# Decode of float64 weights: scales on ScalarE alone, subtracts on VectorE alone, one reduction for the sums of attention weights, and other prices in the planner

## The chip, the core and the metric

The kernel runs on one core of a Trainium2 chip. A core has a matrix engine (TensorE, in rows PE, its weight loads PEld), three engines for elementwise work (VectorE or DVE, ScalarE or ACT, GpSimd or POOL), and an engine that issues transfers (SyncE or SP). Each engine works through its own instructions strictly in order, and waits where an instruction needs the result of another engine or of a transfer. The metric is device microseconds (us) for one execution; lower is better. TensorE's clock has two levels, 1.2 and 2.4 GHz; the profile prints the granted clock as a share of the upper one.

## What is computed

Causal attention with a cumulative bias, then two feed-forward layers over the same 2304 tokens (4 batches of 576):

```
scores = scale * q @ k.T                      # 4 batches, 8 heads, 576 tokens, 64 wide
cum    = cumsum(max(s, 0))
scores = where(causal, -1e9, scores + min(-(cum_i - cum_j), 0))
attn   = exp(scores - max(scores))
attn   = attn / (sum(attn) + 1e-9)
x      = (attn @ v) as (2304, 512)
x      = ((x @ w_a) * (x @ w_b)) @ w_out      # 512 -> 1536 -> 512
out    = (relu(x @ w_in) ** 2) @ w_out2       # 512 -> 2048 -> 512
```

The weights of both layers come as float64. The kernel reads each one as two 32-bit words and makes a float32 pair of it, a high part and a low part.

## The kernel before, in words

All matrix products that need it are made from pairs: high x high, high x low, low x high. That keeps TensorE busy; everything else exists to feed it.

*Decode.* For each tile of 128 x 512 weights a transfer brings 512 KB of raw words (rows `roomxh`, `roomxl`, `words` in the first layer, `v_0r`, `v_1r` in the second). `decode` then scales the high word by 2^-112, shifts it and combines it with its sign (into `t`; rows `roomxl`, `wt`, `v_0t`, `v_1t`), scales the low word by 2^-29, adds both on GpSimd, rounds the sum to the high part (`wh`, `w2h`) on ScalarE, and subtracts that from the sum for the low part (`wl`, `wlo`, `w2l`). Its last argument says which engines may do the subtract: P is GpSimd, D is VectorE. The first layer has 36 such tiles (12 steps f of w_a, w_b and w_out), the second 32. Low parts of the first layer are also written to DRAM (`wlab`, `wlo`) and read back by later chunks (`lo`, `loo`). Raw words of the first 24 tiles rotate through six buffers, those of the last twelve through three.

*Attention.* Batch 0 is done in two parts (256 and 320 queries), the others whole. For each head: scores (`st`), maxima on VectorE (`neg`), exponentials on ScalarE with their sums (`e`, `tot`, in rows `sum`), 1e-9 added and the reciprocal on VectorE (`one`), the weights scaled by it, transposed on TensorE (`pt`), split (`ph`, `pl`) and multiplied with the values (`av`). Where a row of scores lies in two banks, its two sums are added first.

*Feed-forward.* The first layer goes over tokens in chunks; the first chunk (256 tokens) takes its weights directly as they are decoded (`ab`, then `py`). The second layer runs at the end, 512 tokens at a time (`ph`, `po`).

*Order.* `Plan` records every operation with the engines that may do it, a cost for each, and whether it uses the port that VectorE and GpSimd share (third field of a way). `Plan.order` then plays the operations through: for each engine it takes the first startable one by rank (on TensorE attention before feed-forward, elsewhere the reverse), chooses the engine where it can start first, keeps at most one user of the shared port at a time (`port`), and lets the transfers queue up to 3 us ahead of a modelled DMA (`dma`, `QUEUE`). Only the order is emitted; on the chip nothing waits for the planner's times.

Nearly all instructions are issued in line 246, so rows are told apart by their tiles.

Of the kernel before, what the change touches and what calls it, by code (L numbers as in the profile page):

```python
# [248 lines left out]
def attention_moe_moe(tc, q, k, v, s, w_a, w_b, w_out, w_in2, w_out2, out):  # L249
# [73 lines left out]
    def on_dve(method, n, *args, two=False, each=1.04, **kw):  # L323
        return "DVE", 150 + each * n, two, method, args, kw
# [7 lines left out]
    def dve(*args, reads=(), **kw):  # L332
        pl.call(on_dve(*args, **kw), reads=reads)
# [4 lines left out]
    def gps(*args, **kw):  # L338
        pl.call(on_gps(*args, **kw))

    def dma(out, in_, kb, takes=(), lag=0.0):
        pl.call(("SP", kb * 3.0, False, "dma_start", (out, in_), {}), takes=takes, lag=lag)
# [33 lines left out]
    def at_const(shape, dtype, name):  # L376
        v = pl.fixed(lambda: pools["at"].tile(shape, dtype, name=name))
        v.buf.gate = swapped
        return v
# [75 lines left out]
    for i in range(4):  # L455
        t = [at_const([P, NJ + 2], F32, f"{z}{i}") for z in ("neg", "sum", "one")]
        for x in t:
            gps("memset", NJ + 2, x, 1.0)
        small.append(t)
# [110 lines left out]
    def softmax(b, p, h, q0, qn, head):  # L570
# [10 lines left out]
        for i, pieces in enumerate(banks):  # L581
# [53 lines left out]
            for blk, k0, m, to, kn, ee in held:  # L635
                c = blk if k0 == 0 else nq
                n_ = nq + 1 if halves else blk
                act(
                    "activation", kn + 360, ee.part((blk, k0)), to, AF.Exp, bias=neg[:m, n_ : n_ + 1].part(n_),
                    accum_out=tot[:m, c : c + 1].part(c), psum=True,  # L640
                )
            held = []
        if banks[-1][0][1]:
            dve("tensor_reduce", 2, out=tot[:, nq - 1 : nq], in_=tot[:, nq - 1 : nq + 1], op=ALU.add, axis=AX.X)
        qs = slice(first_block, nq)
        dve("tensor_scalar_add", nq, one[:, qs], tot[:, qs], 1e-9)
# [133 lines left out]
    def decode(w, by_col, f, hi, lo, nm, raw, t, takes, by):  # L780
# [5 lines left out]
        else:  # L786
# [7 lines left out]
        pl.call(  # L794
            on_dve("tensor_scalar", n, hf, hf, 2.0**-112, None, op0=ALU.mult, each=0.52),
            on_act("mul", n, hf, hf, 2.0**-112),
        )
        dve("tensor_scalar", n, t, high, 3, 0x7FFFFFF8, op0=ALU.logical_shift_left, op1=ALU.bitwise_and, each=0.52)
        dve("scalar_tensor_tensor", n, t, high, -0x80000000, t, op0=ALU.bitwise_and, op1=ALU.bitwise_or, two=True)
        pl.call(  # L800
            on_act("activation", n, low, low.bitcast(U32), AF.Copy, scale=2.0**-29),
            on_dve("tensor_scalar", n, low, low.bitcast(U32), 2.0**-29, None, op0=ALU.mult, each=0.52),
        )
# [11 lines left out]
    def split_w(f):  # L815
        def g():
# [5 lines left out]
            for i, w in enumerate((w_a, w_b, w_out)):  # L822
# [10 lines left out]
                decode(w, i < 2, f, hi, lo, f"w{f}_{i}", words[k_ % len(words)], t, (), "PD")  # L833
# [275 lines left out]
```

## Time and profile before

| | |
|---|---|
| runs (us) | 1162.74, 1163.14, 1169.74; median 1163.14 |
| profiled execution (us) | 1163.58, its span 1161.8 |
| mean granted clock of TensorE | 0.964 |
| busy TensorE | 1105.1 us (95%) |
| busy VectorE | 670.9 us (58%) |
| busy ScalarE | 494.9 us (43%) |
| busy GpSimd | 324.3 us (28%) |
| transfers | 143.85 MB, mean 124 GB/s |

The span is the time from the first to the last instruction. Busy times are unions; matmuls are pipelined, so a busy TensorE need not be at its peak. Shares over the whole span mix stages: decode and attention of batch 0 first, then attention beside the first layer, then the first layer alone, then the second decode and the second layer. Rows are therefore given by stretches of time. A group's row gives its instructions (x), busy us, mean ns of one, and after the second bar the idle time of the engine just before them with what ended it.

### The profile page before, as it was taken

To read this page: it belongs to the slowest core of one execution; us is meant where nothing else is said; L and a number is where in the kernel's file an instruction comes from. 1 tells how busy PE (TensorE), PEld (TensorE's weight loads), DVE (VectorE), ACT (ScalarE), POOL (GpSimd) and SP (SyncE) were. 2 spreads that over 40 slices of the span, in tenths; PEclk is the share of its full clock that TensorE was granted. 3 is DMA by queue.
4 is the path that set the end of the run, shared out by engine and by line. 5 is a ranking of instruction groups with operands and counts; after the bars stand their busy time and mean duration, and the time that the engine had idled before them with its cause. 6 is when DMAs were issued, how large, how long until landed. Compare 5 with 4: busy or idle time off the path is not lost.

```text
span 1161.8 us, 16590 instructions
## 1 busy us (share of the span) xinstructions
PE 1105.1 (95%) x5888; PEld 969.6 (83%) x5888; DVE 670.9 (58%) x1315; ACT 494.9 (43%) x1164; POOL 324.3 (28%) x284
## 2 busy tenths in 40 slices
PE   5888987699999999999999999998999999999998
PEld 4666666599999999999999999987888888888887
DVE  6778988877888878863232257887232232232232
ACT  5567656557666665442121135455322222222222
POOL 3456655433433342210010036677100010000000
PEclk9689987799999999999999999999999999999999
DMA  6767575664456454335353387653020020010000
GB/s 186 221 187 237 184 219 156 192 175 149 151 170 178 137 158 116 115 100 154 113 164 124 101 271 239 195 175 124 1 73 1 1 73 1 1 55 1 1 37 19
DMA packets 91314, 143.85 MB, mean 124 GB/s; under 512 B 10320, under 2 KB 60240, under 8 KB 91232
## 3 DMA queue, kind: packets, MB, share of 16 engines
q1 hardware_dynamic: 91232, 142.80, 39.9%
q8 instruction: 46, 0.75, 0.3%
q14 instruction: 36, 0.29, 0.1%
HBM read 110.68 MB, written 23.22 MB: 115 GB/s over the span
## 4 chain that ended last, share of the span: by engine, by line
PE 83%; DVE 7%; DMA 5%; issue 1%; POOL 1%; ACT 1%; SPq 0%; DVEq 0%; POOLq 0%; ACTq 0%
PE ab L246 24%; PE po L246 16%; PE ph L246 16%; PE py L246 12%; PE st L246 6%; PE pt L246 5%; PE av L246 5%; DMA loo<-wlo 1%; DVE roomxl L246 1%; DVE neg L246 1%; DVE ph L246 1%; DMA lo<-wlab 1%; DVE one L246 1%; DMA roomxh<-in_moe_w_a 1%; DMA words<-in_moe_w_a 0%
## 5 line engine op out<-in xcount | busy, mean ns | idle before, releaser
L246 DVE SCALAR_TENSOR_TENSOR ph<-ph,r 128x512 f32<-128x512 f32 (+1 forms) x80 | 51.6, 645 | 198.7 <-ACT r L246 198.6
L246 ACT ACTIVATE r<-ph 128x512 f32<-128x512 f32 (+1 forms) x80 | 44.5, 556 | 221.5 <-PE ph L246 221.5
L246 PE MATMUL ab<-xh,wh 128*128 128x432 f32 (+1 forms) x384 | 134.4, 350 | 0.0
L246 PE MATMUL ab<-xl,wh 128*128 128x432 f32 (+1 forms) x384 | 132.7, 346 | 0.0
L246 PE MATMUL ab<-xh,lo 128*128 128x432 f32 (+1 forms) x384 | 132.7, 345 | 0.0
L246 PE MATMUL po<-w2h,g2h 128*128 128x512 f32 x288 | 113.0, 393 | 3.2 <-ACT g2h L246 3.1
L246 ACT ACTIVATE e<-st,neg 128x192 f32<-128x192 f32 (+4 forms) x192 | 92.3, 483 | 54.6 <-DVE neg L246 45.2
L246 PE MATMUL po<-w2l,g2h 128*128 128x512 f32 x288 | 113.0, 392 | 0.0
L246 PE MATMUL po<-w2h,g2l 128*128 128x512 f32 x288 | 112.7, 391 | 0.0
L246 DVE TENSOR_TENSOR ab<-ab,a 128x432 f32<-128x432 f32 (+2 forms) x72 | 40.7, 565 | 113.5 <-PE ab L246 109.4
L246 PE MATMUL pt<-ident,e 128*128 128x128 f32 (+3 forms) x480 | 89.3, 295 | 14.3 <-ACT e L246 5.7
L246 DVE TENSOR_REDUCE neg<-st 128x1 f32<-128x192 f32 (+4 forms) x192 | 79.0, 429 | 16.8 <-PE st L246 13.0
L246 PEld LDWEIGHTS pt<-ident,e 128*128 128x128 f32 (+3 forms) x480 | 57.0, 140 | 34.7 <-ACT e L246 7.6
L246 PE MATMUL py<-gh,wh 128*128 128x432 f32 (+1 forms) x240 | 85.0, 354 | 0.2 <-DVE gl L246 0.2
L246 PE MATMUL py<-gl,wh 128*128 128x432 f32 (+1 forms) x240 | 83.6, 348 | 0.0
L246 PE MATMUL py<-gh,loo 128*128 128x432 f32 (+1 forms) x240 | 83.5, 348 | 0.0
L246 DVE TENSOR_TENSOR g2l<-ph,g2h 128x512 fp32r<-128x512 f32 (+1 forms) x80 | 50.9, 638 | 44.1 <-ACT g2h L246 39.7
L246 ACT COPY a<-ab 128x432 f32<-128x432 f32 (+2 forms) x72 | 34.5, 480 | 93.2 <-PE ab L246 92.9
L246 PEld LDWEIGHTS ab<-xh,lo 128*128 128x128 f32 x384 | 72.2, 188 | 2.2
L246 PEld LDWEIGHTS ab<-xh,wh 128*128 128x128 f32 x384 | 72.4, 189 | 2.0
L246 PEld LDWEIGHTS ab<-xl,wh 128*128 128x128 f32 x384 | 72.4, 189 | 1.9
L246 PE MATMUL av<-ph,vs 128*128 128x320 f32 (+1 forms) x192 | 63.0, 330 | 5.6 <-DVE ph L246 4.7
(214 smaller groups left out, 2820.6 us busy)
## 6 DMA issues: line engine op xcount, KB each, us to landing
lo<-wlab SPq DMA_DIRECT2D x60, 512.0 KB
loo<-wlo SPq DMA_DIRECT2D x48, 384.0 KB
v_0r<-in_moe_w_in SPq DMA_DIRECT2D x16, 512.0 KB
v_1r<-in_moe_w_out SPq DMA_DIRECT2D x16, 512.0 KB
out<-o SPq DMA_DIRECT2D x18, 256.0 KB
roomxh<-in_moe_w_a SPq DMA_DIRECT2D x8, 512.0 KB
roomxh<-in_moe_w_b SPq DMA_DIRECT2D x8, 512.0 KB
roomxl<-in_moe_w_out SPq DMA_DIRECT2D x8, 512.0 KB
```

Of the source, the lines that this page charges most:

```text
L246: getattr(eng, method)(*map(real, args), **{k: real(a) for k, a in kw.items()})
```

## The change

Five edits. (1) `decode` gives both scales to ScalarE alone; before, the planner chose between ScalarE and VectorE. (2) The first layer's subtract goes to VectorE alone ("D"); before, to GpSimd or VectorE ("PD"). The second layer's stays on GpSimd ("P"). (3) The sums of weights get a tile of three columns per block: the sum of the first bank, that of the second bank (0 where there is none), and 1e-9. One reduction over the three columns takes the place of the two-column sum and of the addition of 1e-9. (4) The planner counts VectorE's fast forms (those priced under 1 ns per column) as users of the shared port. (5) The planner prices a transfer at 4.5 instead of 3.0 ns per KB.

```diff
     def on_dve(method, n, *args, two=False, each=1.04, **kw):
-        return "DVE", 150 + each * n, two, method, args, kw
+        return "DVE", 150 + each * n, two or each < 1, method, args, kw
...
     def dma(out, in_, kb, takes=(), lag=0.0):
-        pl.call(("SP", kb * 3.0, False, "dma_start", (out, in_), {}), takes=takes, lag=lag)
+        pl.call(("SP", kb * 4.5, False, "dma_start", (out, in_), {}), takes=takes, lag=lag)
...
-        t = [at_const([P, NJ + 2], F32, f"{z}{i}") for z in ("neg", "sum", "one")]
-        for x in t:
+        t = [at_const([P, *n], F32, f"{z}{i}") for z, n in (("neg", [NJ + 2]), ("sum", [NJ, 3]), ("one", [NJ]))]
+        for x in t[::2]:
             gps("memset", NJ + 2, x, 1.0)
+
+        for c, x in ((0, 1.0), (1, 0.0), (2, 1e-9)):
+            gps("memset", NJ, t[1][:, :, c : c + 1], x)
...
-                    accum_out=tot[:m, c : c + 1].part(c), psum=True,
+                    accum_out=tot[:m, blk, int(c == nq) : int(c == nq) + 1].part(c), psum=True,
...
-        if banks[-1][0][1]:
-            dve("tensor_reduce", 2, out=tot[:, nq - 1 : nq], in_=tot[:, nq - 1 : nq + 1], op=ALU.add, axis=AX.X)
         qs = slice(first_block, nq)
-        dve("tensor_scalar_add", nq, one[:, qs], tot[:, qs], 1e-9)
+        dve(
+            "tensor_reduce", 3 * nq, out=one[:, qs], in_=tot[:, qs], op=ALU.add, axis=AX.X,
+            reads=[tot.part(c) for c in (*range(first_block, nq), *([nq] if banks[-1][0][1] else []))],
+        )
...
-        pl.call(
-            on_dve("tensor_scalar", n, hf, hf, 2.0**-112, None, op0=ALU.mult, each=0.52),
-            on_act("mul", n, hf, hf, 2.0**-112),
-        )
+        act("mul", n, hf, hf, 2.0**-112)
...
-        pl.call(
-            on_act("activation", n, low, low.bitcast(U32), AF.Copy, scale=2.0**-29),
-            on_dve("tensor_scalar", n, low, low.bitcast(U32), 2.0**-29, None, op0=ALU.mult, each=0.52),
-        )
+        act("activation", n, low, low.bitcast(U32), AF.Copy, scale=2.0**-29)
...
-                decode(w, i < 2, f, hi, lo, f"w{f}_{i}", words[k_ % len(words)], t, (), "PD")
+                decode(w, i < 2, f, hi, lo, f"w{f}_{i}", words[k_ % len(words)], t, (), "D")
```

Since the planner's prices change, nearly every engine's order changes. Three places follow. The first is the end of the first decode on VectorE (1295 rows before, 1233 now; a row may stand for several equal instructions). Before, rows 342 to 353:

```order
L246 TENSOR_REDUCE neg_142<-neg_142 128x1
L246 TENSOR_TENSOR wl_2191<-roomxl,wh_0_2179 128x512
L246 SCALAR_TENSOR_TENSOR roomxl<-roomxh,roomxl 128x512
L246 TENSOR_SCALAR roomxl<-roomxl 128x512
L246 TENSOR_SCALAR roomxh<-roomxh 128x512
L246 TENSOR_REDUCE sum_144<-sum_144 128x1
L246 TENSOR_SCALAR one_146<-sum_144 128x5
L246 RECIPROCAL one_146<-one_146 128x5
L246 TENSOR_SCALAR e_1_0_0_1_2081<-e_1_0_0_1_2081,one_146 64x64
L246 TENSOR_SCALAR e_1_0_0_2_2189<-e_1_0_0_2_2189,one_146 128x576
L246 TENSOR_SCALAR e_1_0_0_0_2049<-e_1_0_0_0_2049,one_146 128x320
L246 SCALAR_TENSOR_TENSOR roomxl<-roomxl 128x512
```

Now, rows 229 to 240:

```order
L246 TENSOR_SCALAR roomxl<-roomxl 128x512
L246 TENSOR_TENSOR g_10_1605<-ab_10_1_1566,g_10_1605 128x256
L246 SCALAR_TENSOR_TENSOR roomxl<-roomxl 128x512
L246 TENSOR_REDUCE neg_117<-st_2_256_0_0_1607 64x1
L246 TENSOR_REDUCE neg_117<-st_2_256_0_1_1616 128x1
L246 TENSOR_TENSOR ab_11_1_1620<-ab_11_1_1620,a_11_1611 128x256
L246 TENSOR_REDUCE neg_117<-st_2_256_0_2_1642 128x1
L246 TENSOR_TENSOR wlo_1658<-roomxl,wh_2_1650 128x512
L246 TENSOR_TENSOR g_11_1656<-ab_11_1_1620,g_11_1656 128x256
L246 TENSOR_REDUCE neg_117<-st_2_256_0_3_1652 128x1
L246 TENSOR_REDUCE neg_117<-neg_117 128x1
L246 TENSOR_REDUCE one_123<-sum_127 128x3
```

Before, the decode's last instruction on VectorE stood in row 353, among the heads of batch 1 (`e_1_0`), and the subtract of that last tile followed on GpSimd. Now it is the subtract in row 236, beside the scores of the third pair of heads of batch 0 (`st_2_256`); the scale (`roomxh<-roomxh`) is gone, and the sum, the addition and the reciprocal have become a reduction and a reciprocal.

The second place is TensorE around the last step of the first chunk's `ab` (its matmuls take the tiles that are decoded last). Before, the end of `ab_11_0` and what follows:

```order
L246 MATMUL ab_11_0_2197<-firstgh_404,wh_0_2179 128x256
L246 MATMUL ab_11_0_2197<-firstgl_410,wh_0_2179 128x256
L246 MATMUL ab_11_0_2197<-firstgh_404,wl_2191 128x256
L246 MATMUL st_1_0_1_0_2220<-T_1301 128x320
L246 MATMUL st_1_0_1_0_2220<-t2k_1_1_1818,t2q_1_1_1782 128x320
```

Now:

```order
L246 MATMUL ab_11_0_1588<-firstgh_400,wh_0_1529 128x256
L246 MATMUL ab_11_0_1588<-firstgl_404,wh_0_1529 128x256
L246 MATMUL ab_11_0_1588<-firstgh_400,wl_1545 128x256
L246 MATMUL st_2_256_0_0_1607<-fk_256_1383,fq_85 64x320
L246 LDWEIGHTS mask
L246 MATMUL st_2_256_0_0_1607<-identb,mask 64x64
L246 MATMUL st_2_256_0_1_1616<-fk_256_1383,fq_85 128x448
```

Before, this step stood beside the second pair of heads of batch 1 (`st_1_0_1`); now it stands before the third pair of batch 0. Counted in matmuls of the order, of 5784, the last of `ab_11_1` moved from about the 800th place to about the 569th.

The third place is SyncE's order around the last raw words. Before, from row 159:

```order
L246 DMA val_2_0_1831<-in_v 128x4x128
L246 DMA raw_3q<-in_q 128x576
L246 DMA roomxl<-in_moe_w_out 128x1024
L246 DMA T_1379<-cd 2x576
L246 DMA roomxh<-in_moe_w_a 128x4x256
L246 DMA t2k_2_0_1966<-T_1379 64x576
L246 DMA wlo_1978<-wlo_1955 256x1x128 x2
L246 DMA t2q_2_0_1992<-T_1379 64x576
L246 DMA roomxh<-in_moe_w_b 128x4x256
L246 DMA roomxl<-in_moe_w_out 128x1024
```

Now, from row 115:

```order
L246 DMA roomxl<-in_moe_w_out 128x1024
L246 DMA wlo_1454<-wlo_1444 256x1x128 x2
L246 DMA loo_2_0_1459<-wlo_1157 128x768
L246 DMA roomxh<-in_moe_w_a 128x4x256
L246 DMA roomxh<-in_moe_w_b 128x4x256
L246 DMA loo_2_1_1478<-wlo_1157 128x768
L246 DMA wlab_1502<-wl_1465 128x1024
L246 DMA wlo_1454<-wlo_1506 256x1x128 x2
L246 DMA roomxl<-in_moe_w_out 128x1024
```

The last raw load stood in row 168, behind the loads of three pairs of heads of batch 1 (`raw_3q`); now it stands in row 123, ahead of all of them. The transfers up to it add up to 39.4 MB before and 33.9 MB now, by their shapes.

## Rows read from the trace of the kernel before

**Rows 1.** Busy time by stretch: us from the span's start, length, busy us and instructions (x) of TensorE, its weight loads, VectorE, ScalarE and GpSimd, then granted clock, busy share of the DMA engines, GB/s.

```profile
0.00:232.40 232.40, 184.83 (x934) 140.99 (x935) 189.01 (x392) 138.74 (x352) 121.56 (x117) 0.84 0.64 198
...
87.15:232.40 145.25, 117.82 (x646) 92.94 (x645) 127.72 (x251) 89.74 (x224) 81.68 (x63) 0.84 0.64 198
232.40:522.90 290.50, 288.50 (x1928) 272.38 (x1927) 232.09 (x543) 171.61 (x474) 93.52 (x87) 0.99 0.49 145
522.90:700.00 177.10, 177.10 (x908) 170.23 (x907) 59.56 (x99) 39.72 (x75) 17.75 (x14) 1.00 0.50 155
700.00:800.00 100.00, 96.62 (x458) 86.53 (x457) 79.38 (x109) 51.11 (x90) 69.55 (x51) 0.98 0.60 192
800.00:1161.80 361.80, 358.02 (x1668) 299.43 (x1666) 110.81 (x175) 93.67 (x173) 21.92 (x17) 1.00 0.08 25
```

**Rows 2.** 0 to 232.4 us: TensorE's waits (us in total, times, longest us), and the shares by line of the chain that ended last.

```profile
PE st L246 <- ACT e L246: 12.0, 11, 2.7
PE st L246 <- DMA fk<-cum: 7.9, 1, 7.9
PE av L246 <- DVE ph L246: 6.0, 6, 1.6
...
by line: PE st L246 12.7%; PE ab L246 10.5%; PE pt L246 8.8%; PE av L246 8.7%; DMA loo<-wlo 5.1%; DVE roomxl L246 4.5%; issue 4.2%; PE py L246 3.7%; DVE neg L246 3.4%; DMA roomxh<-in_moe_w_a 2.6%; DVE one L246 2.5%; DVE ph L246 2.5%; DMA wo
```

**Rows 3.** Scales of the decode on VectorE, groups of instructions: the first three in 0 to 232.4 us, the last two in 700 to 800 us.

```profile
L246 DVE TENSOR_SCALAR roomxh<-roomxh 128x512 f32<-128x512 f32 (+1 forms) x12 | 10.6, 887 | 0.9 <-DMA roomxh<-in_moe_w_a 0.9
L246 DVE TENSOR_SCALAR roomxl<-roomxl 128x512 f32<-128x512 f32 (+2 forms) x9 | 6.5, 717 | 0.0
L246 DVE TENSOR_SCALAR words<-words 128x512 f32<-128x512 f32 (+1 forms) x7 | 5.2, 739 | 1.3 <-DMA words<-in_moe_w_a 0.7 <-DMA words<-in_moe_w_out 0.6
...
L246 DVE TENSOR_SCALAR v_1r<-v_1r 128x512 f32<-128x512 f32 (+1 forms) x8 | 6.7, 835 | 1.1 <-DMA v_1r<-in_moe_w_out 1.1
L246 DVE TENSOR_SCALAR v_0r<-v_0r 128x512 f32<-128x512 f32 (+1 forms) x5 | 5.2, 1035 | 0.0
```

**Rows 4.** Scales of the decode on ScalarE in 0 to 232.4 us, the largest group.

```profile
L246 ACT ACTIVATE roomxh<-roomxh 128x512 int32<-128x512 uint32 (+1 forms) x20 | 13.4, 674 | 1.4 <-DMA roomxh<-in_moe_w_a 0.8 <-DMA roomxh<-in_moe_w_b 0.6
```

**Rows 5.** Subtracts of the first decode in 0 to 232.4 us, groups on GpSimd and on VectorE, and the largest group of the decode's additions on GpSimd.

```profile
L246 POOL TENSOR_TENSOR wl<-roomxl,wh 128x512 fp32r<-128x512 f32 x17 | 22.7, 1335 | 16.8 <-ACT wh L246 13.4 <-DVE roomxl L246 1.9 <-DVE wlo L246 1.2
L246 POOL TENSOR_TENSOR roomxl<-roomxl,roomxh 128x512 int32<-128x512 int32 x16 | 21.6, 1350 | 9.5 <-ACT roomxh L246 5.4 <-DVE sum L246 1.9 <-DVE roomxl L246 1.1
...
L246 POOL TENSOR_TENSOR wl<-wt,wh 128x512 fp32r<-128x512 f32 x6 | 7.8, 1299 | 2.2 <-DVE roomxl L246 1.6 <-ACT wh L246 0.4
...
L246 POOL TENSOR_TENSOR wlo<-roomxl,wh 128x512 fp32r<-128x512 f32 x3 | 3.8, 1278 | 4.8 <-ACT wh L246 4.8
L246 POOL TENSOR_TENSOR wlo<-wt,wh 128x512 fp32r<-128x512 f32 x2 | 2.8, 1400 | 2.8 <-ACT wh L246 2.8
...
L246 DVE TENSOR_TENSOR wl<-roomxl,wh 128x512 fp32r<-128x512 f32 x7 | 6.7, 955 | 0.0
```

**Rows 6.** Durations on VectorE by tile over the whole span (ns: least, median, greatest; first and last start): the subtract, the addition of 1e-9, the shift and the combination with the sign; the last row is the same shift as a group, with its busy time.

```profile
L246 DVE TENSOR_TENSOR wl<-roomxl,wh x7: 673/683/1724, 47.7 to 208.7; 128x512 fp32r<-128x512 f32 x7
...
L246 DVE TENSOR_SCALAR one<-sum x40: 151/172/1355, 13.3 to 506.4; 128x5 f32<-128x5 f32 x24, 128x2 f32<-128x2 f32 x8, 128x3 f32<-128x3 f32 x8
...
L246 DVE TENSOR_SCALAR roomxl<-roomxh x16: 406/420/2031, 14.3 to 202.3; 128x512 int32<-128x512 int32 x16
L246 DVE SCALAR_TENSOR_TENSOR roomxl<-roomxh,roomxl x16: 675/684/1715, 17.0 to 209.6; 128x512 int32<-128x512 int32 x16
...
L246 DVE TENSOR_SCALAR roomxl<-roomxh 128x512 int32<-128x512 int32 x16 | 11.0, 689 | 0.6 <-issue 0.6
```

**Rows 7.** Sums of weights and reciprocals on VectorE as groups in 0 to 232.4 us, and the reductions of scores by tile over the whole span (ns: least, median, greatest).

```profile
L246 DVE TENSOR_SCALAR one<-sum 128x2 f32<-128x2 f32 (+2 forms) x20 | 11.0, 551 | 0.4 <-POOL firstgl L246 0.2
...
L246 DVE RECIPROCAL one<-one 128x2 f32<-128x2 f32 (+2 forms) x20 | 3.3, 167 | 0.2
L246 DVE TENSOR_REDUCE sum<-sum 128x1 f32<-128x2 f32 x12 | 1.7, 142 | 0.0
...
L246 DVE TENSOR_REDUCE neg<-st x192: 175/448/626, 9.9 to 503.0; 128x1 f32<-128x288 f32 x64, 128x1 f32<-128x448 f32 x32, 128x1 f32<-128x192 f32 x24, 128x1 f32<-128x320 f32 x24
L246 DVE TENSOR_REDUCE neg<-neg x32: 136/155/156, 50.0 to 503.9; 128x1 f32<-128x2 f32 x32
```

**Rows 8.** Timeline (start us, us): SyncE's issues of the last raw loads, and the last subtract of the first decode on GpSimd.

```profile
138.13 0.39 SPq L246 DMA_DIRECT2D roomxh<-in_moe_w_a  x1
...
158.87 0.54 SPq L246 DMA_DIRECT2D roomxh<-in_moe_w_a  x1
...
182.10 0.38 SPq L246 DMA_DIRECT2D roomxh<-in_moe_w_a  x1
...
194.39 0.35 SPq L246 DMA_DIRECT2D roomxl<-in_moe_w_out  x1
...
221.16 1.29 POOL L246 TENSOR_TENSOR wlo<-roomxl,wh 128x512 fp32r<-128x512 f32 x1 [4.37 <-ACT wh L246]
```

**Rows 9.** Timeline of GpSimd at the start: one of the memsets of the small tiles.

```profile
5.43 0.10 POOL L246 MEMSET sum<- 128x7 f32 x1
```

## The prediction

> **What bounds the kernel now.** I read the busy time by stage first. Between 232.4 and 700 us TensorE is busy for 288.5 of 290.5 us and then for all of 177.1, at a granted clock of 0.99 to 1.00; from 800 us to the end it is busy for 358.0 of 361.8 [rows 1]. Nothing that VectorE, ScalarE or GpSimd give up there can shorten the kernel. What can be won lies in two places. In 0 to 232.4 us TensorE is busy for 184.8 us, so 47.6 us are idle, and its granted clock there is 0.84 on average [rows 1], a mean of its two levels, 1.2 and 2.4 GHz; work that arrives more densely would be paid back at the higher level as well. In 700 to 800 us 3.4 us are idle. Next I asked who is late in the first stage. TensorE's waits are many and short, none of them large: ScalarE's exponentials 12.0 us in 11 waits, one transfer 7.9 us once, VectorE's ph 6.0 us [rows 2]. There is no single stall to remove. The chain of that stretch is mixed in the same way, TensorE, VectorE and transfers in turn [rows 2]. Of the engines that feed TensorE, VectorE is the fullest: 127.7 of 145.25 us (88%) in 87 to 232 us, against 62% on ScalarE and 56% on GpSimd; the transfers hold 0.64 of the DMA engines [rows 1]. So I price the change in VectorE time within the first 232 us.
>
> **The change, part by part.** *Scales.* In the first stage 28 of the 72 scale instructions of the decode ran on VectorE, for 10.6 + 6.5 + 5.2 = 22.3 us; in 700 to 800 us 13 did, for 11.9 us [rows 3]. All go to ScalarE. There one takes 0.674 us [rows 4], so ScalarE gets 28 x 0.674 = 18.9 us more in the first stage: 138.7 + 18.9 = 157.6 of 232.4 us, 68%. That is cover enough unless the exponentials queue behind the scales, which is a rival below.
>
> *Subtracts.* 17 + 6 + 3 + 2 = 28 of the 36 ran on GpSimd, for 22.7 + 7.8 + 3.8 + 2.8 = 37.1 us, and all 36 are now VectorE's [rows 5]. The price on VectorE lies between 0.683 us, the median of the seven that were there, and 0.955 us, their mean, which a single one of 1.724 us pulls up [rows 5, 6]. GpSimd will be less busy, which speaks for the median, but VectorE and GpSimd still alternate in each word of the decode, which speaks for the mean. I take 0.82: 28 x 0.82 = 23.0 us added (19.1 to 26.7).
>
> *Sums of weights.* In the first stage 20 additions of 1e-9 take 11.0 us and 12 two-column sums 1.7 us; one 3-column reduction for each of the 20 heads takes their place [rows 7]. The trace has no such reduction. The nearest rows are the two-column minimum, 0.136 us at least, and the smallest reduction of scores (64 columns), 0.175 us [rows 7]. I take 0.16: 20 x 0.16 = 3.2 us (2.7 to 3.5). The gain is 12.7 - 3.2 = 9.5 us. Most of it is not work: the same addition takes 0.151 us at least, 0.172 in the median and 1.355 at most [rows 6]. The reciprocal, which stays, does not show this (0.167 us on average) [rows 7].
>
> *Waits on the port.* The shifts show two levels too, 0.420 us in the median and 2.031 at most; 16 of them take 11.0 us where 16 x 0.42 = 6.7 would do (the combinations with the sign likewise, 0.684 and 1.715) [rows 6]. Something blocks them for 4.3 us, and GpSimd's instructions, 1.3 us each [rows 5], have about that length. With 37.1 us less of GpSimd's 121.6 and a planner that keeps such pairs apart I take half, 2.2 us (0 to 4.3).
>
> The Trainium skill (SBUF — State Buffer, "SBUF: two separate sides") says that VectorE and GpSimd share one pair of ports under an exclusive lock, taken for the whole instruction, by a VectorE instruction in a two-port mode or with two SBUF inputs. The two levels above agree. By that rule the moved subtract, with two inputs in SBUF, needs the lock too, so the move also adds candidates for blocking; if the rule bit every time, the sum would be that of the port rival below.
>
> First stage by VectorE's load: -22.3 + 23.0 - 9.5 - 2.2 = -11.0 us (from -4.8 with the dear ends to -17.5 with the cheap ones).
>
> *Order.* The planner's new prices reorder nearly everything, and the order of the rows gives a second count. Before, the last word of the decode leaves GpSimd at 221.16 + 1.29 = 222.5 us [rows 8], and TensorE's last matmul of the first chunk's ab stands about 800th of 5784 in its order; now it stands about 569th. So 231 matmuls, those of four heads of batch 0 and of nearly four of batch 1, move behind the decode. At the pace of the full stage, 288.5 us / 1928 = 0.150 us [rows 1], they cost 231 x 0.150 = 35 us later, when TensorE runs without gaps. The change therefore gains if the decode ends before 222.5 - 35 = 187 us. On VectorE the last word of the decode stood in row 353 of its order and stands in row 236 now. At 222.5 / 353 = 0.63 us per row that is 149 us. This is the low end, since 108 of the 236 rows are now shifts, combinations and subtracts of the decode; if every row were as long as the 0.82 us of the moved subtract, it would be 194 us. I take 170, about the middle, and by this count the gain is 187 - 170 = 17 us. Little VectorE work shares that stretch, so the chain within a word (load, ScalarE, VectorE, GpSimd, ScalarE, VectorE) is less well covered than before. I therefore take 13 us, between the two counts and nearer the first. The moved heads need VectorE afterwards, where it is busy for 232.1 of 290.5 us [rows 1]: 58 us of slack hold them.
>
> *Second decode (700 to 800 us).* VectorE gives up 11.9 of its 79.4 us [rows 1, 3]; ScalarE has 51.1 and takes 13 x 0.674 = 8.8. TensorE idles for 3.4 us, which is the most to be had; I take 1.5. Its subtracts stay on GpSimd.
>
> *The DMA price* changes no transfer, only their order; its cost is the transfer rival. The eight more memsets at the start, 0.1 us each [rows 9], lie on GpSimd ahead of the first weights' sums, while the first scores are still being made, at no cost; in the open they would cost 0.8 us.
>
> The profiled execution took 1163.6 us around its span of 1161.8, and the median of the runs is 1163.1, so both are the same base. Sum: 1163.6 - 13 - 1.5 = 1149 us.
>
> **The rivals.** *Relief that does not arrive* (no change). ScalarE's exponentials are TensorE's largest wait already [rows 2], and ScalarE is given 18.9 us in the same queue. Each exponential may then stand behind a scale of 0.674 us. For it: the waits are short and mixed, so relief of one engine can be eaten by the next. Against it: ScalarE stays at 68%. Only the second decode's part would be left, 1163.6 - 1.5 = 1162 us.
>
> *Transfers set the pace of the decode* (slower). By the shapes in the DMA queue's order 39.4 MB go out before the end of the last raw load, and 33.9 MB now. At 198 GB/s, the mean of the first stage [rows 1], that is 199 us before (it was issued at 194.39 [rows 8]) and 171 now: the load moves up by 28 us, and so does the end of the decode, to 194.5 to 199 us. It would come 8 to 12 us after the 187 at which the moved matmuls are paid for. For it: the last loads of w_a, with three buffers only, followed each other by 20.7 and 23.2 us (138.13, 158.87, 182.10) [rows 8]. Against it: the DMA engines are busy for 0.64 only, and loads then waited for buffers that a crowded VectorE freed late. Time: 1163.6 + 12 - 1.5 = 1174 us. It decides if the last raw load goes out after 187 - 28 = 159 us.
>
> *The port* (slower). Each of the 28 moved subtracts meets an instruction of GpSimd and takes 1.724 us, as the longest did [rows 6]: 28 x (1.724 - 0.82) = 25 us more, 1149 + 25 = 1174 us. Against it: the median is 0.683 us, while GpSimd was busier than it will be. It decides from a mean of about 1.3 us.
>
> **How the numbers follow.** The forecast (VectorE's relief arrives; 1132 to 1160, its own range) has 0.55, of which 0.42 lies over 1% under the time before and 0.13 within 1%, about what a measurement of this kernel can tell from no change. Relief that does not arrive has 0.25, all within 1%. Transfers have 0.15 and the port 0.05, both over 1% slower. So: faster 0.42, same 0.38, slower 0.20. The range runs from 1132 us (the order's 17 us, the cheap ends and a clock that recovers with denser work) to 1174 us, the middle of the slow cases, half of which lie above it.
>
> **What would show it.** Right: the last subtract of the decode before 187 us, at 165 to 175; TensorE idle for under 40 us in the first 232 us or full well before 232; no scale on VectorE; VectorE's subtract at 0.68 to 0.95 us on average; the reduction of the weights' sums at 0.14 to 0.18 us and never above 0.5; 232 to 700 us as full as before. Wrong: exponentials that wait on ScalarE behind scales, with TensorE's wait for them above 20 us; raw loads after 159 us; a subtract with a mean above 1.3 us; or gaps in TensorE after 232 us, because the moved heads find no cover.

## The result, and the profile after

The changed kernel takes 1182.46 us (median of 4 runs, 1180.86 to 1184.1), the kernel before beside it 1163.9 us (4 runs): ratio 1.0149, 95% interval 1.0115 to 1.0182. The forecast was 1149 us. It is slower, and above the range.

The busy time by stretch of the kernel after, with the columns of [rows 1], and two stretches that [rows 1] does not have, 0 to 100 and 800 to 825 us:

```profile
0.00:100.00 100.00, 75.56 (x301) 54.65 (x302) 61.89 (x146) 63.32 (x158) 28.36 (x52) 0.83 0.62 190
0.00:232.40 232.40, 182.80 (x870) 136.86 (x870) 150.28 (x332) 142.29 (x343) 68.75 (x83) 0.84 0.64 196
87.15:232.40 145.25, 119.07 (x618) 90.21 (x617) 96.70 (x207) 88.88 (x208) 44.86 (x35) 0.84 0.66 202
...
700.00:800.00 100.00, 95.45 (x466) 87.08 (x464) 60.88 (x91) 56.01 (x100) 55.45 (x41) 1.00 0.57 185
800.00:825.00 25.00, 16.08 (x60) 13.06 (x61) 13.80 (x18) 12.82 (x23) 15.73 (x12) 0.73 0.40 126
800.00:1179.10 379.10, 366.37 (x1692) 306.14 (x1692) 118.09 (x182) 107.29 (x198) 35.38 (x27) 0.98 0.10 31
```

The same two added stretches of the kernel before:

```profile
0.00:100.00 100.00, 79.86 (x374) 58.52 (x375) 72.35 (x163) 58.65 (x152) 49.65 (x62) 0.86 0.68 208
800.00:825.00 25.00, 25.00 (x112) 20.71 (x111) 12.51 (x17) 11.50 (x20) 14.11 (x11) 1.00 0.20 63
```

In the first 232.4 us VectorE's busy time falls from 189.01 to 150.28 us and GpSimd's from 121.56 to 68.75, far more than the forecast's sum. Part of that fall is heads' work that now comes after 232.4 us (332 instructions on VectorE instead of 392); the order-kept run f_both below shows the fall without it, 18 us. TensorE does not use the room: 182.80 us and 870 matmuls, against 184.83 and 934 [rows 1]; it idles for 49.6 us, where under 40 was forecast. From 232.4 to 700 us TensorE is as full as before (464.8 of 467.6 us), as forecast. A second loss stands late, where the kernel before has a full TensorE: 8.9 of 25 us idle after 800 us, at a granted clock of 0.73, between the two levels.

The single operations came out as priced. VectorE's subtract and the new reduction by tile (ns: least, median, greatest):

```profile
L246 DVE TENSOR_TENSOR wl<-roomxl,wh x24: 673/685/1390, 27.9 to 166.8; 128x512 fp32r<-128x512 f32 x24
...
L246 DVE TENSOR_REDUCE one<-sum x40: 142/160/174, 13.1 to 533.6; 128x5 f32<-128x15 f32 x24, 128x2 f32<-128x6 f32 x8, 128x3 f32<-128x9 f32 x8
```

The subtracts as groups in 0 to 232.4 us (count, busy us, mean ns), against [rows 5]:

```profile
L246 DVE TENSOR_TENSOR wl<-roomxl,wh 128x512 fp32r<-128x512 f32 x24 | 17.1, 717 | 4.9 <-ACT wh L246 4.9
...
L246 DVE TENSOR_TENSOR wl<-wt,wh 128x512 fp32r<-128x512 f32 x6 | 4.9, 821 | 0.1
...
L246 DVE TENSOR_TENSOR wlo<-wt,wh 128x512 fp32r<-128x512 f32 x3 | 2.5, 829 | 1.9 <-ACT wh L246 1.8
...
L246 DVE TENSOR_TENSOR wlo<-roomxl,wh 128x512 fp32r<-128x512 f32 x3 | 2.1, 689 | 0.8 <-ACT wh L246 0.8
```

The 36 subtracts take 26.6 us, 0.74 us each. The timeline gives the last raw load of the first decode and its last subtract, against [rows 8]:

```profile
157.67 0.55 SPq L246 DMA_DIRECT2D roomxl<-in_moe_w_out  x1
...
172.83 0.68 DVE L246 TENSOR_TENSOR wlo<-roomxl,wh 128x512 fp32r<-128x512 f32 x1
```

So the decode ends at 173.5 us, 49 us earlier than before, and inside the forecast's 165 to 175. TensorE's waits in 0 to 232.4 us, against [rows 2]:

```profile
PE st L246 <- ACT e L246: 11.8, 11, 2.3
PE py L246 <- DMA loo<-wlo: 10.1, 2, 6.6
PE pt L246 <- ACT e L246: 7.8, 7, 2.4
PE st L246 <- DMA fk<-cum: 7.8, 1, 7.8
```

One wait is new: `py` for `loo`, low parts of w_out that have just been written to DRAM and are read back. Here the two waits end at 152.5 and 159.7 us; in the kernel before it is 0.3 us in this stretch. What TensorE lacks by then shows in the transfers' queue, here some issues of raw words in 60 to 126 us, and the issues of q and v on either side of them:

```profile
61.85 0.51 SPq L246 DMA_DIRECT2D fq<-in_q  x1
...
67.17 0.38 SPq L246 DMA_DIRECT2D words<-in_moe_w_a  x1
68.41 0.33 SPq L246 DMA_DIRECT2D roomxl<-in_moe_w_out  x1
...
74.59 0.56 SPq L246 DMA_DIRECT2D words<-in_moe_w_b  x1
...
120.54 0.56 SPq L246 DMA_DIRECT2D roomxl<-in_moe_w_out  x1
...
125.58 0.45 SPq L246 DMA_DIRECT2D val<-in_v  x1
```

From 62 to 125 us no q, k or v goes out. The kernel before issues 13 rows of them there, the first and the last being:

```profile
66.71 0.52 SPq L246 DMA_DIRECT2D fk<-in_k  x1
...
113.26 0.47 SPq L246 DMA_DIRECT2D fq<-in_q  x1
```

TensorE's gap after 795 us (timeline: start, us, and in brackets what it waited for), then the chain that ended last there:

```profile
795.06 0.39 PE L246 MATMUL ph<-yhy,w2l 128*128 128x512 f32 x1
808.92 0.80 PE L246 MATMUL po<-w2h,g2h 128*128 128x512 f32 x1 [13.47 <-ACT g2h L246]
```

```profile
796.12 0.70 DVE ph L246
...
798.10 1.29 POOL v_1t L246
799.39 0.02 issue
799.40 3.61 DMA v_0r<-in_moe_w_in
...
803.12 0.68 ACT v_0r L246
...
806.45 1.29 POOL v_0t L246
...
807.77 0.62 ACT w2h L246
808.38 0.49 ACT g2h L246
```

The cast `g2h` needs only `ph`, ready at 796.8 us. It runs at 808.4, because ScalarE's queue has scales of raw words ahead of it, and one waits for a load that left at 799.40, when GpSimd had freed its buffer. The rounding `w2h` of the same word stands ahead of the cast too, and waits until 807.74 us for GpSimd's addition (`v_0t`). In the kernel before the cast comes right behind a scale that waits for its load:

```profile
791.11 0.66 ACT L246 ACTIVATE v_0r<-v_0r 128x512 f32<-128x512 f32 x1 [1.33 <-DMA v_0r<-in_moe_w_in]
791.67 1.54 ACT L246 CAST g2h<-ph 128x512 fp32r<-128x512 f32 x3
```

The span is 17.3 us longer (1179.1 against 1161.8). The second layer's first matmul (`ph`) starts at 758.0 us instead of 752.0: 6.0 us from the first half. The wait in front of `po` is 13.5 us instead of 3.1: 10.4 us more.

### The profile page after: what moved, and what is told of

Its sections match the earlier page's. It is cut to its first block, busy times and chain, and to the rows that moved or that the text cites. A ratio compares the mean times of both kernels' runs of the same rounds, so it can differ in the third digit from the quotient of the medians.

```text
span 1179.1 us, 16556 instructions
## 1 busy us (share of the span) xinstructions
PE 1109.4 (94%) x5888; PEld 972.2 (82%) x5888; DVE 621.6 (53%) x1261; ACT 531.8 (45%) x1232; POOL 260.5 (22%) x246
## 4 chain that ended last, share of the span: by engine, by line
PE 89%; DVE 4%; ACT 3%; DMA 1%; issue 1%; POOL 1%; SPq 0%; DVEq 0%; POOLq 0%; ACTq 0%
PE ab L246 25%; PE po L246 17%; PE ph L246 17%; PE py L246 13%; PE st L246 6%; PE av L246 6%; PE pt L246 6%; ACT e L246 1%; DVE roomxl L246 1%; DVE neg L246 1%; DMA loo<-wlo 1%; DVE ph L246 0%; ACT wh L246 0%; ACT roomxh L246 0%; SPq L246 0%
## 5 line engine op out<-in xcount | busy, mean ns | idle before, releaser
L246 PE MATMUL po<-w2h,g2h 128*128 128x512 f32 x288 | 113.5, 394 | 13.5 <-ACT g2h L246 13.5
L246 PEld LDWEIGHTS po<-w2h,g2h 128*128 128x128 f32 x288 | 54.8, 190 | 25.1 <-ACT g2h L246 14.3
```

Source lines behind the costliest of these rows:

```text
L246: getattr(eng, method)(*map(real, args), **{k: real(a) for k, a in kw.items()})
```

## The experiments

Most kernels use one device: the change's rules by half. The first set holds up to the end of attention (`swap`), the second from there on; a rule that is missing is as in the kernel before. The new sums of weights stay or go with the first half as told.

```diff
+    rules = set(FIRST)
...
-        return "DVE", 150 + each * n, two or each < 1, method, args, kw
+        return "DVE", 150 + each * n, two or ("port" in rules and each < 1), method, args, kw
...
-        pl.call(("SP", kb * 4.5, False, "dma_start", (out, in_), {}), takes=takes, lag=lag)
+        pl.call(("SP", kb * (4.5 if "dma" in rules else 3.0), False, "dma_start", (out, in_), {}), takes=takes, lag=lag)
...
     pl.add({"CTL": (0.0, [(swap, (), {})], False)}, [swapped], [])
+    rules.clear()
+    rules.update(SECOND)
```

`scales` and `sub` choose between the two forms of `decode` in the same way. ALL stands for the four rules. Where a price changes, the planner also divides the work anew among the engines that may do it. Two figures of the orders are used: the **place** of the last `ab` matmul of the first chunk, its row in TensorE's order (weight loads have rows, equal neighbours share one, so 786 and 542 rows stand for the 800th and 569th matmul), and the **words**, the rows of shifts and combinations of the second decode that stand ahead of the first `g2l` on VectorE.

**Which half loses.**

```diff
+    FIRST, SECOND = ALL, {}        # s1_after_s2_before, new sums
+    FIRST, SECOND = {}, ALL        # s1_before_s2_after, old sums
+    FIRST, SECOND = {}, {"scales"} # s2_scales, old sums
+    FIRST, SECOND = {}, {"dma"}    # s2_dma, old sums
```

> All edits of the change up to the end of attention, the rules of before from there on (both engines may scale in the second decode, old port rule and old transfer price). Theory A: the loss has two parts, 6 us in the first stage and 11 us in the second decode, where a product for TensorE's last layer waits on ScalarE behind a scale that waits for its raw load. Then this gives 1163.9 + 6 = 1170 us and a wait of TensorE's po for ScalarE under 4 us. Rival B: the second stall only follows from the first stage's order; then it stays near 1182 us with a stall over 10 us.

> The rules of before up to the end of attention, all edits of the change from there on. Theory A: 1163.9 + 11 = 1175 us, with a wait of TensorE's po for ScalarE's cast of 10 us or more. Rival B: 1164 us, no such wait.

> Before, with one edit alone: in the second decode ScalarE makes both scales; prices of the planner as before. Theory A: this edit is the cause of the second part, 1172 to 1175 us and a wait of TensorE's po for ScalarE of 10 us. Rival C: the dearer transfers in the planner are (raw loads stand later); then 1164 us here.

> Before, with one edit alone: from the end of attention on the planner prices transfers at 4.5 instead of 3.0 ns per KB. Theory A: 1164 us, po's wait under 4 us. Rival C (dearer transfers put the raw loads later and so cause the second part): 1172 to 1175 us with a wait of 10 us.

Measured, beside 1165.22 us for the kernel before: 1174.38 (1.0074, 1.0044 to 1.0104); 1176.65 (1.0103, 1.0079 to 1.0127); 1160.17 (0.9961, 0.9943 to 0.9978); 1173.43 (1.009, 1.0058 to 1.0121). Both halves lose. In the second the price alone is enough; more scales on ScalarE, which I had suspected, measure 0.4% faster, no more than a price without meaning gives below.

**Which edit loses in the first half.**

```diff
+    FIRST, SECOND = {"dma"}, {}    # s1_dma, old sums
+    FIRST, SECOND = {"sub"}, {}    # s1_sub, old sums
+    FIRST, SECOND = {"scales"}, {} # s1_scales, old sums
+    FIRST = SECOND = {"port", "scales", "sub"} # a_nodma, new sums
```

> The kernel before with one edit, for the first half alone: the planner prices transfers at 4.5 instead of 3.0 ns per KB up to the end of attention, and at 3.0 from the second decode on. In TensorE's order the last matmul of the first chunk's ab on weights of the decode moves from place 786 to 490 (542 with all edits). Theory D (the transfer price reorders the first half, and heads that leave the decode without cover cost more later than the earlier decode gives): slower, 1170 to 1178 us, at least as much as the first half of the change with all edits (+0.74%). Theory E (the loss of the first half comes from operations bound to one engine, subtracts on VectorE or scales on ScalarE): within 3 us of before.

> The kernel before with one edit: the first layer's subtracts on VectorE alone. Place of the last ab matmul 654 instead of 786. Theory D: the loss goes with the place, so less than half of s1_dma's: 1164 to 1169 us. Theory E: slower, 1170 us or more. The prediction's own reason (VectorE's load counts, 28 x 0.82 = 23 us more on it): about 1163 + 23 = 1186 us, if nothing is taken off VectorE in exchange.

> The kernel before with one edit: the first decode's scales on ScalarE alone. Place of the last ab matmul 766 instead of 786, so hardly any reordering of TensorE. Theory D: within 4 us of before. Theory E: slower, 1168 us or more. The prediction's own reason (22.3 us off a VectorE that bounds the stage): 1163 - 22 = 1141 us.

> The kernel after with one edit undone in both halves: the planner prices transfers at 3.0 ns per KB. Place of the last ab matmul 681. Theory D: the 11 us of the second decode come back (the transfers of raw words go out early again) and most of the first half's 8.6 us: 1160 to 1168 us. Theory E: only the 11 us come back: 1171 to 1173 us. The prediction's own reason without its transfer rival: 1149 us.

Measured, beside 1164.53: 1198.59 (1.0307, 1.027 to 1.0345); 1151.8 (0.9904, 0.9869 to 0.9938); 1172.09 (1.0069, 1.0041 to 1.0097); 1156.73 (0.9929, 0.9905 to 0.9953). The price alone costs 34 us, nearly twice the loss of the whole change and well over the 1170 to 1178 us expected. Taking it out of the kernel after (a_nodma) gives back 26 us, more than the loss. The stretch and the wait of s1_dma:

```profile
0.00:100.00 100.00, 58.49 (x272) 49.49 (x273) 75.11 (x140) 53.86 (x125) 44.43 (x56) 0.73 0.67 210
```

```profile
PE py L246 <- DMA loo<-wlo: 22.1, 3, 14.4
```

With heads missing, TensorE is busy for 58.49 of the first 100 us and follows the decode to the read-back. The single edits do not follow the forecast's count: the subtracts, priced there at 23 us more on VectorE, gain 1%, and the scales, priced at 22 us less, lose 0.7%. VectorE's busy time in 0 to 232.4 us is lower in both (177.33 and 172.73 us), since the order changes with them. Neither theory of these expectations has both: the subtracts gained where D had no gain and E a loss, and the scales lost as E said. And one expectation of mine for a_nodma fell: the second layer starts at 737.8 us, but the wait in front of `po` stays, 11.3 us. Without the price, the port rule (beside the scales) still leaves 33 words ahead instead of 37.

**The cause in the first half.** On TensorE the planner ranks attention ahead of the feed-forward, on every other engine, SyncE's queue too, behind it. My reading: with dear transfers its model's queue is always full, and decode and weights, ranked first, take each slot. The next two put attention first in that queue and keep 4.5; beside them the version without the price and with the scales alone in the second decode, and a price that means nothing.

```diff
-    RANK = {"PE": {"first": 0, "att": 1, "moe": 2, "late": 3}, "any": ...}
+    RANK = {"SP": {"first": 0, "att": 1, "moe": 2, "late": 3}, "PE": ..., "any": ...}
...
+    FIRST = SECOND = ALL           # a_sp_att, with the rank, new sums
+    FIRST, SECOND = {"dma"}, {}    # s1_dma_sp_att, with the rank, old sums
+    FIRST, SECOND = {"port", "scales", "sub"}, {"scales"} # s1_nodma_s2_scales, new sums
+    FIRST, SECOND = {"dma"}, {}    # s1_dma31, 3.1 for 4.5, old sums
```

> The kernel after, price 4.5 kept, with one edit: for transfers alone the planner ranks attention ahead of the feed-forward, as it does on TensorE; before, everywhere else the feed-forward comes first. 61 loads of q, k and v stand ahead of the last raw load of the decode (61 before, 39 after), the last ab matmul at place 772 (786 before, 542 after). Theory S (with dear transfers the model's queue is always full, and the decode's loads, ranked first, keep out those of attention, so TensorE has no heads to work on): TensorE busy 78 us or more in the first 100 us, no wait of py for loo above 1 us, entry into the second layer at 738 to 750 us instead of 758; the second decode's stall stays (29 words): 1159 to 1171 us. If the loss has another cause (the price's effect on anything but those loads): 1176 us or more.

> The kernel before with the price 4.5 in the first half (1198.6 us by itself) and the same rank for transfers, attention first. 67 loads of q, k and v ahead of the last raw load, last ab matmul at place 819. Theory S: the 34 us come back, 1158 to 1170 us, TensorE busy 78 us or more in the first 100 us instead of 58.5. Otherwise: 1185 us or more.

> All edits but the transfer price (3.0 throughout), and from the second decode on only the scales on ScalarE: no port rule there. In VectorE's order 37 shifts and combinations of the second decode stand ahead of the first g2l, as in the kernel before (37) and the one with the scales alone (37); the three kernels that stall there have 29, 31 and 33. Theory H (TensorE's first po waits behind raw words that the order puts ahead of the cast g2h, and the fewer words are done by then the longer): no wait above 4 us there, entry into the second layer at 738 us as without the price, and 1161.8 - 14 - 3 = 1143 to 1147 us. If the gain of the first half came from elsewhere, or the stall has nothing to do with the words: 1155 us or more.

> The kernel before with a price of 3.1 instead of 3.0 in the first half: a change that means nothing by itself but makes another order (last ab matmul at place 745). It measures what any reordering does. Theory N (orders differ by chance, so that the -1% of the subtracts and the +0.7% of the scales alone need no cause): it may lie anywhere within 1% of before, and more than 0.4% away from it. If orders this close are worth the same: within 0.4%.

Measured, beside 1164.85: 1163.48 (0.9975, 0.995 to 1.0001); 1183.78 (1.0145, 1.0103 to 1.0188); 1144.97 (0.9798, 0.9747 to 0.9849); 1161.47 (0.9956, 0.993 to 0.9982). With the rank alone the kernel after comes back by 19 us at the full price; its first 100 us:

```profile
0.00:100.00 100.00, 78.11 (x320) 52.77 (x321) 68.20 (x160) 67.64 (x171) 30.98 (x56) 0.81 0.64 197
```

The wait for `loo` is gone, the second layer starts at 741.2 us, and the second decode's wait stays at 13.6 us, all as expected. With the price alone the rank gives back only 15 of 34 us: TensorE is about as busy as before at first (78.26 of 100 us), but now heads keep back the decode, whose last subtract ends at 245.8 us. That expectation was missed.

**Load with the order kept.** The planner plans as before, but the instructions are emitted on the other engine at the same place; the orders of TensorE and of the transfers are those of the kernel before, row for row. A fourth kernel has a second price without meaning.

```diff
-            eng = self.engine.get(op.eng)
-            for method, args, kw in op.ways[op.eng][1]:
+            by = op.force or op.eng
+            eng = self.engine.get(by)
+            for method, args, kw in op.ways[by][1]:
...
+        pl.force = "ACT" if by == "PD" else None # around each scale: f_scales, f_both
...
+        pl.force = "DVE" if by == "PD" else None # around the subtract: f_sub, f_both
...
+    FIRST, SECOND = {"dma"}, {} # s1_dma29, 2.9 for 4.5, old sums
```

> The kernel before with its order kept, row for row, on TensorE and in the transfers' queue: the planner plans as before, but the first layer's 28 subtracts that it gave to GpSimd are emitted on VectorE, at the same place in the plan. So only the engine's load changes, not the order. Theory V (VectorE bounds the first half, the prediction's count): +23 us on VectorE, so slower by 10 us or more, 1175 us and up. Theory G (GpSimd is the late one in the decode's chain, since each of its subtracts takes 1.3 us and stands ahead of the next word's addition; that is why the subtracts alone gained 1%): faster by 0.4% or more, 1152 to 1160 us. Theory O (the gain came from the new order): within 0.4%.

> The kernel before with its order kept, the 28 scales of the first decode that the planner gave to VectorE emitted on ScalarE. Theory V: 22 us less on VectorE, so faster by 5 us or more: 1142 to 1158 us. Theory A (ScalarE's queue matters more than VectorE's load; the scales alone lost 0.7%): slower by 0.4% or more. Theory O: within 0.4%.

> The kernel before with its order kept and both moved: scales on ScalarE, subtracts on VectorE. VectorE's load changes by -22 + 23, about nothing; GpSimd's by -37 us, ScalarE's by +19. Theory V: within 0.4% of before. Theory G: faster, and more so than the subtracts alone if VectorE's load matters too: 1146 to 1158 us. Theory O: within 0.4%.

> The kernel before with a price of 2.9 instead of 3.0 per KB in the first half: a second reordering that means nothing by itself (last ab matmul at place 680; 3.1 gave 0.9956). If places below some 700 cost by themselves: slower, 1168 us or more. Chance of the order alone: within 1% to either side.

Measured, beside 1164.81: 1167.43 (1.0023, 1.0003 to 1.0043); 1163.65 (0.9994, 0.9975 to 1.0012); 1166.76 (1.0023, 1.0002 to 1.0044); 1150.82 (0.9887, 0.9847 to 0.9927). The first 232.4 us of f_sub, f_scales and f_both:

```profile
0.00:232.40 232.40, 181.64 (x939) 138.75 (x940) 196.09 (x422) 138.81 (x354) 90.81 (x91) 0.86 0.64 199
```

```profile
0.00:232.40 232.40, 187.28 (x934) 141.98 (x935) 171.58 (x367) 151.74 (x377) 123.55 (x117) 0.83 0.63 197
```

```profile
0.00:232.40 232.40, 187.39 (x911) 141.95 (x912) 170.98 (x375) 145.65 (x359) 84.13 (x87) 0.85 0.60 188
```

With the order kept, 17 us less on VectorE gain nothing (f_scales, the run that tells the forecast's count from an effect of the order alone), 18 us less on VectorE and 37 less on GpSimd gain nothing either (f_both), and 7 us more on VectorE cost next to nothing (f_sub). Nor does ScalarE eat the relief in f_scales: TensorE's waits for it come to 17.9 us, against 20.0 before. A price of 2.9, which adds and removes no work, gains 1.1%; in its new plan 21 of the 36 subtracts are VectorE's, 8 before.

**The form of the price's cost.**

```diff
+    FIRST, SECOND = ALL, {"scales"} # s1_p400_s2_scales, 4.0 for 4.5, new sums
+    FIRST, SECOND = {"port", "scales", "sub"}, {"scales"} # n_sp_att, with the rank, new sums
```

> The version that was fastest so far (all edits of the first half, scales alone in the second) with the transfer price at 4.0 instead of 3.0 per KB in the first half. 55 loads of q, k and v stand ahead of the decode's last raw load (57 at 3.0, 39 at 4.5), the last ab matmul at place 646 (681 at 3.0, 542 at 4.5). Theory S (the price costs only where it keeps the heads' loads out): 1139 to 1152 us, like the version at 3.0 (1145). If the price costs in proportion (two thirds of the 29 us between 1145 and the 1174 of the first half at 4.5): 1158 to 1168 us.

> The fastest version so far (price 3.0) with attention ranked first among transfers: 54 loads of q, k and v ahead of the last raw load, last ab matmul at place 648. At this price the model's queue has room for both, so the rank should be worth little. Theory S: 1139 to 1152 us. If attention first gains by itself: under 1139 us.

Measured, beside 1164.59: 1138.4 (0.9777, 0.9747 to 0.9808) and 1147.68 (0.9857, 0.9829 to 0.9885). The cost does not grow in proportion to the price. At 4.0, with 55 loads ahead, it is absent (1138.4 us is just under the range expected); at 4.5, with 39, it is there. So it sets in between, together with the loss of those loads. At 4.0 this kernel beats both the one before and the one after. The rank gains nothing by itself.

The kernels with different first halves, from the profiles, by the end of the decode (last subtract), with the start of the second layer:

| kernel | place | decode ends, us | second layer starts, us |
|---|---|---|---|
| s1_dma | 490 | 169.3 | 781.9 |
| s1_after_s2_before | 542 | 170.9 | 763.6 |
| after | 542 | 173.5 | 758.0 |
| s1_p400_s2_scales | 646 | 185.5 | 728.3 |
| s1_nodma_s2_scales | 681 | 190.2 | 727.2 |
| n_sp_att | 648 | 192.0 | 739.4 |
| s1_dma29 | 678 | 195.5 | 734.7 |
| a_nodma | 681 | 199.4 | 737.8 |
| s1_sub | 654 | 200.4 | 744.4 |
| a_sp_att | 772 | 216.3 | 741.2 |
| f_sub | 786 | 220.9 | 750.3 |
| before | 786 | 222.5 | 752.0 |
| f_scales | 786 | 223.2 | 752.5 |
| s1_dma31 | 745 | 223.3 | 753.5 |
| s1_scales | 764 | 227.5 | 760.1 |
| f_both | 786 | 231.1 | 761.7 |
| s1_dma_sp_att | 819 | 245.8 | 774.8 |

(The expectations gave 766 and 680 as the places of s1_scales and s1_dma29; the orders have 764 and 678.) The profiled run of s1_nodma_s2_scales lies 9.5 us under its median, that of f_both 7.6 us over, and the first half of s1_nodma_s2_scales is that of a_nodma; so rows here carry some 10 us of scatter. The ends of the series stand out all the same: 727 to 744 us where the decode ends at 185 to 200 us, 758 us and more where it ends by 174, and 750 us and more from 220 on (a_sp_att, at 216, still has 741). These kernels differ in more than this one figure, so the table shows a pattern and not its cause.

The same for the second decode: 37 words ahead go with waits of 1.2 to 3.2 us in front of the first `po` (before 3.1, s1_after_s2_before 3.2, s2_scales, s1_nodma_s2_scales, n_sp_att and s1_p400_s2_scales 1.2), 33 with 11.3 (a_nodma), 31 with 13.6 (s2_dma), 29 with 13.5 and 13.6 (after, s1_before_s2_after, a_sp_att). s1_nodma_s2_scales was expected to be free of the wait on this ground, and was.

## Why the prediction was wrong

**"The DMA price changes no transfer, only their order; its cost is the transfer rival": this step failed.** The order was the cost. In the first half the price kept q, k and v out of the queue for 64 us (61.85 to 125.58); by itself it costs 34 us, and the rank alone, at the same price, brings the kernel after back by 19. In s1_dma the rank gives back only 15 of the 34, so the late loads are not the whole of the price's cost there; what the rest is stays open. I had counted which matmuls move behind the decode, but took it that TensorE would have something else to do meanwhile. I looked at the order of TensorE and VectorE, and in the transfers' queue only at raw words.

**The break-even of 187 us was mis-sized.** The decode ends 49.0 us earlier than before, yet the second layer starts 6.0 us later: what moved behind the decode cost 49.0 + 6.0 = 55.0 us, where I took 35. That puts the break-even at 222.5 - 55 = 167.5 us, which the last subtract at 173.5 does not reach. The stretch from the end of the decode to the second layer, in the kernels before, after and a_sp_att, gives the parts:

```profile
222.50:752.00 529.50, 522.99 (x3129) 496.56 (x3129) 342.63 (x721) 243.66 (x615) 147.85 (x128) 0.99 0.52 158
```

```profile
173.50:758.00 584.50, 572.10 (x3385) 530.53 (x3386) 359.10 (x796) 289.89 (x739) 147.08 (x131) 0.99 0.49 152
```

```profile
216.30:741.20 524.90, 523.73 (x3134) 498.86 (x3133) 304.71 (x668) 252.95 (x633) 134.45 (x119) 0.99 0.49 156
```

Of the 55.0 us, 572.10 - 522.99 = 49.1 are TensorE's busy time on 256 more matmul records, 0.19 us each, and 5.9 are idle time. Against a_sp_att the same sum gives 42.8 + 16.8 = 59.6 us: 48.4 busy and 11.2 idle. The price of 0.150 was the mean of a full stage; the matmuls that moved came from the first stage, whose own row gives 184.83 / 934 = 0.198 [rows 1]. The idle time had no term.

**VectorE as the bound of the first half: this fell.** With the order kept, 17 us less on VectorE gave 0.9994, and 18 us less 1.0023. The row that misled is its 88% in 87 to 232 us [rows 1]: it was the fullest, but TensorE's waits did not single it out. Over 0 to 232.4 us they come to 15.7 us for VectorE, all groups together, 20.0 for ScalarE and 8.9 for transfers; [rows 2] has only the longest groups, and I let the share decide. In f_both, with 18 us less on VectorE, TensorE's waits for it rise to 21.2 us. The kernel after without the price (a_nodma, 1156.73 us) does lie in the forecast's own range, but not for its reason, so the size of the 13 us was met by chance: by the ratios the first half without the price is worth 0.9798/0.9961, 1.6% or 19 us, but a price of 2.9 with no edit gives 1.1%. How much of the 1.6% the edits themselves earn stays open; single edits of -1.0% (subtracts) and +0.7% (scales) are hardly larger than what an order without meaning does (-0.4 and -1.1%).

**The terms of VectorE's sum** were near for each instruction (subtract 0.74 us for 0.82, reduction 0.160 for 0.16), as was the decode's end (173.5 us for 170). The scales were miscounted: 25 of the first decode ran on VectorE, for 19.8 us, and not 28 for 22.3. One row of [rows 3] mixes forms, and three of its nine instructions are shifts, which stay; by form the row has

```profile
L246 DVE TENSOR_SCALAR roomxl<-roomxl 128x512 int32<-128x512 int32 x3 | 2.5, 819 | 0.0
```

The waits on the port were put too small: 2.2 us, at most 4.3. In f_sub all subtracts on VectorE rise from 7.4 to 29.6 us, 22.2 more, but its busy time by only 196.09 - 189.01 = 7.1. The groups of its other instructions, in the same order and with two more of them in the stretch, come to 189.3 us instead of 200.6, so some 11 us left them (15 by the busy time, in which overlaps count once). The Trainium skill (SBUF — State Buffer, "SBUF: two separate sides") has the pair of ports as an exclusive lock between VectorE and GpSimd for a whole instruction; that taking 28 instructions off GpSimd shortens those of VectorE agrees with it. The port rival (1.724 us per subtract) is refuted by the mean of 0.74.

**Second decode, "I take 1.5":** it lost 10.4 us. I priced it by load, with 3.4 us of idle time as the most to be had, and named no wait. The place was in the trace: the kernel before waits 3.1 us for `g2h` behind the same scales. Price and port rule each put fewer words ahead. That the cast stands behind a scale that waits for its load, and behind the rounding of that word, is read from the chain; that the wait goes with the words holds in the eleven kernels named above, and was forecast for one of them. It wasn't tried to move the cast alone, so the words as the cause are argued.

**The rivals.** Transfers: its 1174 us came near, but not its mechanism. The last raw load left at 157.67 us, before the 159 that would decide; the raw words were early and the heads' inputs late. Relief that does not arrive: f_scales and f_both show it (no gain from an emptier VectorE), though not through the exponentials: TensorE's `st` waits for them 11.5 and 10.4 us there, 11.8 in the kernel after and 12.0 before.

## What to carry to other kernels

A planner's price is an edit to every queue: before costing it, list for each queue which class of work goes out in which stretch, the transfers' queue first, and ask what the bound engine has left to do there. The fullest engine is not the bound until a change of its load alone, with the order kept, moves the time. And where an order comes from a list of prices, time a few prices that mean nothing; a gain smaller than theirs belongs to no edit.

## What was not expected of the hardware

TensorE's gap costs more than its length. After it the matmuls stand 0.43 us apart for 5 us, then 0.23; the kernel after, timeline of TensorE:

```profile
809.52 0.63 PE L246 MATMUL po<-w2l,g2h 128*128 128x512 f32 x1
809.94 0.63 PE L246 MATMUL po<-w2h,g2l 128*128 128x512 f32 x1
...
814.18 0.40 PE L246 MATMUL po<-w2h,g2h 128*128 128x512 f32 x1
814.41 0.40 PE L246 MATMUL po<-w2l,g2h 128*128 128x512 f32 x1
```

The granted clock in the gap, in the first work after it, and in the stretch that follows:

```profile
795.50:808.90 13.40, 0.00 (x0) 0.00 (x0) 8.18 (x9) 8.19 (x15) 10.23 (x8) 0.69 0.43 134
808.90:816.00 7.10, 7.08 (x20) 5.59 (x21) 4.97 (x7) 4.55 (x8) 4.54 (x5) 0.63 0.40 129
816.00:825.00 9.00, 9.00 (x41) 7.47 (x40) 4.47 (x7) 3.52 (x7) 3.21 (x3) 1.00 0.23 72
```

The clock fell while TensorE stood, and 0.63 is a mean of the two levels: the lower one, 1.2 GHz, lasted into the new work. Twelve matmuls at 0.20 us more are 2.4 us on top of the 13.5.

VectorE's instructions grow shorter when GpSimd's are taken away: with 28 subtracts gone from GpSimd (f_sub), some 11 us over 232 us, at the same order.
